# A transformer block on one core: products by half rows, a ninth window slot, a bf16 residual, another start, and an order of issue with tasks that stand back

## The chip, the cores and the metric

The kernel runs on one core of a Trainium2 chip. The core's engines run side by side, each with its own queue of instructions: TensorE (PE, matrix products, with PEld its loading of weights), VectorE (DVE), ScalarE (ACT), GpSimd (POOL) and SyncE (SP, which here issues most of the DMA transfers). The metric is the device time of one execution in microseconds (us). The change is compared with the kernel before by that time.

## The reference, cut to what matters

One block: layer norm, attention over eight earlier positions two apart, output projection and residual, then layer norm, a GELU MLP, bias and residual. The sequence has S = 2048 rows of D = 576 values, 32 heads of 18, and the MLP is F = 4608 wide. All inputs and the output are bf16.

```python
qkv = (ln(x) @ wqkv) -> q, k, v            # (S, 32, 18) each
off = arange(8) * 2                         # this position and 7 earlier ones, 2 apart
logits = einsum("bhsd,bhswd->bhsw", q, k[s - off]) * 18 ** -0.5   # -1e9 where s - off < 0
o = einsum("bhsw,bhswd->bhsd", softmax(logits), v[s - off])
h = x + o @ wo
out = h + gelu(ln(h) @ w1 + b1) @ w2 + b2
```

## The kernel before

**Tiling.** The 2048 rows are cut into 16 tiles of 128: tile j holds the rows p*16 + j, partition p. A step of two positions is therefore a step of two tiles, and a window of eight reaches over all tiles of the same parity, those with a higher j shifted by one partition. The tiles are worked on in the list `ORDER`: the eight even j from 14 down, then the eight odd ones; n is the place in this list.

**Stages of tile n.** `front(n)`: sums for the layer norm (`ln1a`, DVE), the reciprocal root by a power on POOL (`ln1r`), normalisation (`ln1b`, on DVE for n < 8, on ACT after that), transposition (`t1` on PE and `t1e` as copy by ACT for n < 8, `t1e` as DMA transpose on SP's queue after that), then three products with `wqkv` (`c{n}K`, `c{n}V`, `c{n}Q`; line 392), evicted from PSUM by ACT (`e{n}K` ...; line 405) into the windows `kwin[e]`, `vwin[e]` (eight slots for each parity e) or into a `q` buffer. D = 576 is four blocks of 128 rows and a fifth with 64 live rows, the other 64 being zero: a product is 2 halves x 5 blocks = 10 matmuls of 288 columns. K and V of a tile are also written to DRAM (`bw`, lines 425 and 426) and read back one partition lower (`ks`, `vs`, lines 520 and 522) once the tile's own p1a and p2a are done.

`attention(n)` is DVE's: `p1a` (q times the window, line 444), `p1s`, `p1t` and `p1b` (sums over a head, maximum over the slots in three steps, difference), `ex` (ACT's exponential), `p2n` (sum over slots in three steps, reciprocal, weights), `p2a`, `p2s`, `p2b` (weights times values, summed into `o`).

`project(n)`: o is transposed (`t2`: for n < 3 by PE in nine transposes and a copy, otherwise by two DMA transposes on SP's queue), multiplied with `wo` (18 matmuls of 64 rows, two of which run side by side; line 564), evicted as f32 `h`, x is added to it and its sums are taken (`ln2a`), `hb` = h + b2 is put away in bf16, h is normalised on ACT (`ln2b`) and transposed again (`t3`).

`mlp(g)` handles two tiles at once: nine units `u{g}.{u}` on PE (36 matmuls of 64 rows and 256 columns, in pairs; line 630), GELU on ACT (line 641), then four passes of 36 matmuls of 128 rows, `m{g}.{a}.{half}.{u}` in pieces of four (line 667, tile `po`), and `out` on DVE (line 686) with the store `st`. The page names a matmul's shape by its rows: 128*128 or 64*128.

**What sets the order.** Nothing is issued as it is written down. Every step is given to a planner, `Weaver` (line 16), by `add` with its engine, an assumed cost, the steps it comes after, a priority, and buffers that it takes and gives back. `run` (line 35) goes through a simulated time: it always issues next the step that could start earliest, and among equals the one of the lowest priority. So the program is one fixed list for each engine, and an engine does not go past an instruction that waits. PSUM has two buffers for `po` and three (two banks each) for all else.

**The start.** DVE clears the padding of x, of wqkv's last block and of a row of DRAM (lines 274 to 278). Eleven matmuls on idle data (`warm`) come first on PE. The xT tiles lie in parts of the windows that are still free.

Of the kernel before, what the change touches and what calls it, by code (L numbers as in the profile page):

```python
# [15 lines left out]
class Weaver:  # L16
# [4 lines left out]
    def __init__(self, slots):  # L21
        self.tasks = {}
        self.slots = {tag: [0.0] * n for tag, n in slots.items()}
        self.held = {}

    def add(self, name, engine, cost, fn, after=(), prio=0.0, take=None, give=(), lag=0.1, table=None, kb=0.0,
            backlog=2.5, transfers=1):
        assert name not in self.tasks, name
        self.tasks[name] = (engine, cost, fn, tuple(after), prio, take, tuple(give), lag, table,
                            (kb, backlog, transfers))  # L30


    RATE, TABLE, LANES = 240.0, 1.28, 8

    def run(self):
# [8 lines left out]
        table, queue, landed = None, 0.0, [0.0] * self.LANES  # L44
        while left:
            best = None
            for n in ready:
                engine, cost, fn, after, prio, take, give, lag, tab, (kb, backlog, transfers) = left[n]
                start = max([clock.get(engine, 0.0)] + [done[a][2 if done[a][0] == engine else 1] for a in after])
                if take is not None:  # L50
                    tag, key = take
                    if key not in self.held:
                        if not self.slots[tag]:
                            continue
                        start = max(start, min(self.slots[tag]))
                if kb:
                    start = max(start, queue - backlog, landed[transfers - self.LANES - 1])
                rank = (round(start, 3), prio, n)
# [3 lines left out]
            start, _, n = best  # L62
            engine, cost, fn, after, prio, take, give, lag, tab, (kb, backlog, transfers) = left.pop(n)
            ready.discard(n)
            if take is not None and take[1] not in self.held:
                tag, key = take
                free = min(self.slots[tag])
                self.slots[tag].remove(free)
                self.held[key] = tag
            fn()  # L70
            if tab is not None and tab != table:
                cost += self.TABLE
                table = tab
# [8 lines left out]
            for key in give:  # L82
                self.slots[self.held.pop(key)].append(done[n][1])
# [7 lines left out]
def kernel(  # L91
# [37 lines left out]
    dram = ctx.enter_context(tc.tile_pool(name="dram", bufs=1, space=bass.MemoryType.DRAM))  # L129
    ps_po = ctx.enter_context(tc.tile_pool(name="ps_po", bufs=2, space=bass.MemoryType.PSUM))  # L130
    ps_pm = ctx.enter_context(tc.tile_pool(name="ps_pm", bufs=3, space=bass.MemoryType.PSUM))

    kvd = dram.tile([NT, P + 1, 2 * D], BF16, name="kvd")
# [15 lines left out]
    kwin = [wpool.tile([P, W, D], BF16, name=f"kwin{e}") for e in range(2)]  # L149
    vwin = [wpool.tile([P, W, D], BF16, name=f"vwin{e}") for e in range(2)]  # L150
# [10 lines left out]
    def late_pool():  # L161
        if not late:
# [4 lines left out]
    HB, HT, LG, NQ = 4, 9, 4, 13  # L167
# [3 lines left out]
    wv = Weaver({"po": 2, "pm": 3, "oT": 1, "h": 2, "xr": 2, "hb": HB,  # L171
                 "hT": HT, "osb": 2, "hnT": 2, "lg": LG, "prod": 1, "q": NQ})
    add = wv.add
# [3 lines left out]


    TP, TO = 8, 3
    SLACK = 0.6  # L180
    WARM = 11
# [9 lines left out]
    def x_load(n):  # L191
        def fn():
            nc.sync.dma_start(out=T["x", n][:, 0:D], in_=x3[:, ORDER[n], :])
        return fn
# [8 lines left out]
    def wq_rest(eng, t):  # L203
        return lambda: eng.dma_start(out=wqkv_sb[0:64, 4, t * D:(t + 1) * D], in_=A_wqkv[512:576, t * D:(t + 1) * D])
# [30 lines left out]
    Q, K, V = 0, 1, 2  # L235
    for n in range(NT):
        if n < LENT:
            T["x", n] = kwin[1][:].rearrange("p w c -> p (w c)")[:, n * DP:(n + 1) * DP]
        elif n < LENT + XH:
            T["x", n] = hn_bufs[0][:].rearrange("p a b -> p (a b)")[:, (n - LENT) * DP:(n - LENT + 1) * DP]  # L240
        else:
            T["x", n] = early.tile([P, DP], BF16, name=f"x{n}")[:]
        load(f"x{n}", x_load(n), 147, prio=0.1 * n if n else -300)
    for t in (K, V, Q):
        eng, at = (nc.scalar, -200) if t == K else (nc.sync, 0.55 if t == Q else 0.75)
        for r, (part, fn, kb) in enumerate((("a", wq_load(eng, t, 0, 2), 295), ("b", wq_load(eng, t, 2, 4), 295),
                                            ("c", wq_rest(eng, t), 74))):
            add(f"W{t}{part}", "ACT" if t == K else "SP", 0.5, fn, (), at + 0.01 * r, lag=1.8, kb=kb)

    def b2_load():  # L250
        nc.sync.dma_start(out=b2_bc[:], in_=B_b2.partition_broadcast(P))
        nc.sync.dma_start(out=kvd[:, 0, :], in_=w2_sb[0:NT, 0:2, :].rearrange("p a c -> p (a c)"))

    load("b2", b2_load, 150, prio=8.5, issue=0.7, transfers=2)
# [6 lines left out]
    for c in range(W1C):  # L261
        for half in range(2):
            for k in range(0, KC, W1K):
                bulk(f"w1{c}{half}{k}", w1_chunk(c, half, k), 295, prio=20 + c)
    for c in range(W2C):
        bulk(f"w2{c}", w2_chunk(c), 295, prio=30 + c, after=("b2", "b1t", "warm"))
# [5 lines left out]

    for n in range(NT):
        nc.vector.memset(T["x", n][:, D:DP], 0.0)
        if n in (1, 3, 5):
            t = (K, V, Q)[n // 2]
            nc.vector.memset(wqkv_sb[64:128, KT - 1, t * D:(t + 1) * D], 0.0)
    nc.vector.memset(w2_sb[0:NT, 0:2, :], 0.0)


    def warm():
        pw = ps_pm.tile([P, 1024], F32, tag="pm", name="warm")
# [3 lines left out]
    add("warm", "PE", 5.0, warm, (), -400, take=("pm", "warm"), give=("warm",))  # L286

    def b1_turn():
        T["b1T"] = ps_pm.tile([P, 2048], BF16, tag="pm", name="b1T")[:, 0:FT]
# [26 lines left out]
    def transposed(src, shifted=False):  # L316
        starts = [kt * P for kt in range(KT)] + ([64 + kt * P for kt in range(KT - 1)] if shifted else [])
        pt = ps_pm.tile([P, 2048], BF16, tag="pm", name="pt")[:, 0:len(starts) * P]
        pt = pt.rearrange("p (k t) -> p k t", t=P)
        for k, c0 in enumerate(starts):  # L320
            nc.tensor.transpose(pt[:, k, :], src[:, c0:c0 + P], ident[:])
        return pt

    def region(n):
        return n if n < LENT else (0, 1, 2, 3, 0, 1, 0)[n - LENT]


    def front(n):  # L330
# [3 lines left out]
        def ln1a():  # L334
            ln_stats(L1, n, T["x", n][:, 0:D])
            if n >= W:
                ln_var(nc.vector, L1, n, (1.0, EPS))

        def ln1r():
            if n < W:  # L340
# [6 lines left out]
        def ln1b():  # L347
            if n < W:
                nc.vector.tensor_scalar(out=T["x", n][:, 0:D], in0=T["x", n][:, 0:D], scalar1=L1["mv"][:, n, 0:1],
                                        scalar2=L1["rs"][:, n, :], op0=ALU.subtract, op1=ALU.mult)  # L350
            else:
                nc.scalar.activation(out=T["x", n][:, 0:D], in_=T["x", n][:, 0:D], func=ACT.Identity,
                                     scale=L1["rs"][:, n, :], bias=nmr[:, n, :])

        def t1():
            T["pt1", n] = transposed(T["x", n])

        def t1e(by_dma=False):
            if n < 2 * LENT:
                flat = (vwin if n < LENT else kwin)[1][:].rearrange("p w c -> p (w c)")  # L360
                r = region(n)
                T["xnT", n] = flat[:, r * DP:(r + 1) * DP].rearrange("p (k t) -> p k t", k=KT)
            else:
                T["xnT", n] = early.tile([P, KT, P], BF16, name=f"xnT{n}")[:]
            if by_dma:
                nc.sync.dma_start(out=T["xnT", n], in_=T["x", n], transpose=True)
            else:
                nc.scalar.copy(out=T["xnT", n], in_=T["pt1", n])  # L368
# [330 lines left out]
    for g in range(len(GROUPS)):  # L699
        mlp(g)  # L700
# [32 lines left out]
```

## Time and profile before

| | |
|---|---|
| median of 3 runs | 382.62 us (382.17 to 382.9) |
| the profiled execution | 382.82 us, of which its span is 381.0 us |
| PE busy | 373.8 us, 98% of the span |
| DVE busy | 292.5 us, 77% |
| ACT busy | 209.0 us, 55% |
| DMA | 38.48 MB, mean 101 GB/s |
| granted PE clock | 1.00 |

The profile comes from one execution, taken by the hardware. A row gives start, busy time, engine, line of the code, and the tiles written and read; what stands in square brackets is the time that the engine stood idle before it, with what ended it. Matmuls are pipelined and the busy time of a merged row has the drain of its last matmul in it; so the time that a run of matmuls takes on PE is read from its start to the start of the next row. Lines of the chain give start, length and what ran, without brackets. In group rows the numbers after the bar are busy us, mean ns of one, idle us before, and what ended that.

### The profile page before, as it was taken

How to read it: one execution, taken by the hardware profiler on the slowest of the kernel's cores; microseconds unless marked ns; L12 is line 12 of the kernel's file. 1: busy time of each engine (PE TensorE's matmuls, PEld its weight loads, DVE VectorE, ACT ScalarE, POOL GpSimd, SP SyncE). 2: the span in 40 equal slices, each digit the busy share in tenths (PEclk: the TensorE clock that was granted, in tenths of full speed). 3: DMA queues.
4: the chain of work that ended last, by engine and by line, in shares of the span. 5: the costliest groups of instructions: out<-in, count | busy, mean ns of one | idle time of the engine just before them, and what ended most of it. 6: DMA issues, size and time to landing. Idle time of an engine off the chain costs nothing.

```text
span 381.0 us, 10766 instructions
## 1 busy us (share of the span) xinstructions
PE 373.8 (98%) x4618; PEld 304.8 (80%) x4618; DVE 292.5 (77%) x563; ACT 209.0 (55%) x437; POOL 32.4 (9%) x55
## 2 busy tenths in 40 slices
PE   7999999999999999999999999999999999999996
PEld 3777787788788887887788778877887788778874
DVE  7999999899999999999999899998968932010000
ACT  2896665888255762575257526870685088106700
POOL 3670011000110110010001100110011011000000
PEclk9999999999999999999999999999999999999999
DMA  8798999986523212352232333222313331000000
GB/s 254 229 193 273 211 226 236 308 270 199 99 48 101 69 22 64 50 80 62 48 94 64 49 77 82 48 65 61 80 41 56 93 80 25 11 15 19 2 17 15
DMA packets 63967, 38.48 MB, mean 101 GB/s; under 512 B 39520, under 2 KB 63904, under 8 KB 63920
## 3 DMA queue, kind: packets, MB, share of 16 engines
q1 hardware_dynamic: 63296, 37.13, 41.4%
q8 instruction: 36, 0.59, 0.6%
q10 hardware_dynamic: 624, 0.66, 0.5%
q14 instruction: 11, 0.09, 0.1%
HBM read 22.28 MB, written 6.52 MB: 76 GB/s over the span
## 4 chain that ended last, share of the span: by engine, by line
PE 72%; DVE 14%; DMA 2%; issue 1%; POOL 0%; ACT 0%; DVEq 0%; ACTq 0%
PE po L667 35%; PE pm L630 33%; PE pw L564 4%; DVE prod L444 3%; DVE prod L450 2%; DVE prod L485 2%; DMA kwin<-kvd 2%; DVE prod L491 1%; DVE l_st L306 1%; DVE prod L495 1%; DVE h L577 1%; DVE half L437 0%; DVE half L438 0%; DVE hb L590 0%; DVE lg L457 0%
## 5 line engine op out<-in xcount | busy, mean ns | idle before, releaser
L641 ACT ACTIVATE hT<-pm,b_sb 128x256 bf16<-128x256 f32 x288 | 112.5, 477 | 88.6 <-PE pm L630 88.3
L630 PE MATMUL pm<-hnT,w_sb 64*128 64x256 bf16 x2592 | 144.7, 269 | 0.0
L667 PE MATMUL po<-w_sb,hT 128*128 128x288 bf16 x1152 | 142.9, 286 | 0.0
L630 PEld LDWEIGHTS <-w_sb 64*128 64x128 bf16 x2592 | 125.7, 94 | 17.1 <-issue 1.8
L667 PEld LDWEIGHTS <-hT 128*128 128x128 bf16 x1152 | 111.9, 98 | 29.9 <-issue 2.0
L686 DVE TENSOR_TENSOR osb<-po,hb 128x288 bf16<-128x288 f32 x32 | 14.2, 453 | 56.0 <-PE po L667 56.0
L314 POOL TENSOR_TENSOR l_rs<-l_ve,mhalf 128x1 f32<-128x1 f32 x32 | 27.0, 844 | 277.8 <-DVE l_ve L310 277.2
L450 DVE TENSOR_TENSOR prod<-prod 128x2304 bf16<-128x2304 bf16 (+1 forms) x64 | 44.1, 690 | 1.5
L444 DVE TENSOR_TENSOR prod<-kwin,q 128x4608 bf16<-128x4608 bf16 x16 | 40.9, 2555 | 1.3 <-DMA kwin<-kvd 0.9
L485 DVE TENSOR_TENSOR prod<-vwin,at 128x4608 bf16<-128x4608 bf16 x16 | 40.9, 2554 | 0.5 <-ACT vwin L405 0.2
L594 ACT ACTIVATE hn<-h,nmr,l_rs 128x576 bf16<-128x576 f32 (+1 forms) x32 | 19.2, 652 | 23.1 <-issue 13.3
L392 PE MATMUL pq<-wqkv_sb,vwin 128*128 128x288 bf16 x210 | 27.5, 286 | 1.4 <-ACT vwin L368 0.8
L392 PE MATMUL pq<-wqkv_sb,kwin 128*128 128x288 bf16 x210 | 27.1, 286 | 0.0
L392 PEld LDWEIGHTS <-vwin 128*128 128x128 bf16 x210 | 20.1, 98 | 6.9 <-ACT vwin L368 1.2
L392 PEld LDWEIGHTS <-kwin 128*128 128x128 bf16 x210 | 20.2, 98 | 5.4 <-issue 0.5
L491 DVE TENSOR_TENSOR prod<-prod 128x2304 bf16<-128x2304 bf16 x16 | 21.7, 1358 | 0.6
L564 PE MATMUL pw<-wo_sb,oT 64*128 64x288 bf16 x288 | 20.3, 283 | 0.0
L577 DVE TENSOR_TENSOR h<-h,xr 128x576 f32<-128x576 f32 x16 | 12.0, 753 | 10.4 <-ACT h L569 10.4
L569 ACT COPY h<-pw 128x576 f32<-128x576 f32 x16 | 10.5, 654 | 15.4 <-PE pw L564 15.4
L564 PEld LDWEIGHTS <-oT 64*128 64x128 bf16 x288 | 13.6, 94 | 4.3 <-issue 1.2
L405 ACT CAST vwin<-pq 128x576 bf16<-128x576 f32 x16 | 10.2, 641 | 6.9 <-PE pq L392 6.9
L405 ACT CAST kwin<-pq 128x576 bf16<-128x576 f32 x16 | 10.2, 639 | 6.3 <-PE pq L392 6.3
(63 smaller groups left out, 224.8 us busy)
## 6 DMA issues: line engine op xcount, KB each, us to landing
w_sb<-in_B_w_dram SPq DMA_DIRECT2D x36, 288.0 KB, 5.7
xr<-in_A_x_dram SPq DMA_DIRECT2D x16, 144.0 KB, 2.3
out_dram<-osb SPq DMA_DIRECT2D x16, 144.0 KB, 1.9
kvd<-kwin SPq DMA_DIRECT2D x14, 144.0 KB, 4.4
kvd<-vwin SPq DMA_DIRECT2D x14, 144.0 KB, 4.0
kwin<-kvd SPq DMA_DIRECT2D x14, 144.0 KB, 3.0
vwin<-kvd SPq DMA_DIRECT2D x14, 144.0 KB, 2.1
wqkv_sb<-in_A_wqkv_dram SPq DMA_DIRECT2D x4, 288.0 KB, 5.6
```

The source lines that it names most:

```text
L314: nc.gpsimd.tensor_tensor(out=L["rs"][:, n, :], in0=L["ve"][:, n, :], in1=mhalf[:], op=ALU.pow)
L392: nc.tensor.matmul(pq[:, p0:p0 + HALF], lhsT=T["xnT", n][:, kt, :], rhs=wqkv_sb[:, kt, c0:c0 + HALF], start=(kt == 0), stop=(kt == KT - 1))
L405: nc.scalar.copy(out=dst.rearrange("p (d h) -> p d h", h=H), in_=src.rearrange("p h d -> p d h"))
L444: nc.vector.tensor_tensor(out=prod[:], in0=kwin[e][:], in1=T["q", n][:].unsqueeze(1).to_broadcast([P, W, D]), op=ALU.mult)
L450: nc.vector.tensor_tensor(out=pv[:, :, 0:b - a, :], in0=pv[:, :, 0:b - a, :], in1=pv[:, :, a:b, :], op=ALU.add)
L485: nc.vector.tensor_tensor(out=prod[:].rearrange("p w (d h) -> p w d h", d=Dh, h=H), in0=vwin[e][:].rearrange("p w (d h) -> p w d h", d=Dh, ...
L491: nc.vector.tensor_tensor(out=prod[:, 0:4, :], in0=prod[:, 0:4, :], in1=prod[:, 4:8, :], op=ALU.add)
L564: nc.tensor.matmul(pw[:, half, 0:HALF], lhsT=T["oT", n][lo:lo + 64, block(c, half), :], rhs=wo_sb[lo:lo + 64, c, :], start=(c == 0), stop= ...
L594: nc.scalar.activation(out=hn_slots[n % 2][:, c0:c1], in_=src, func=ACT.Identity, scale=L2["rs"][:, n, :], bias=nmr[:, n, :])
L630: nc.tensor.matmul(pm[:, half, q, 0:width], lhsT=w1_sb[lo:lo + 64, c, f0:f0 + P], rhs=T["hnT", g][lo:lo + 64, block(c, half), 0:width], st ...
L641: nc.scalar.activation(out=T["hT", g, u][:, half, q, 0:width], in_=T["pm", g, u][:, half, q, 0:width], func=ACT.Gelu_apprx_tanh, bias=b1_s ...
L667: nc.tensor.matmul(T["po", n, half][:], lhsT=T["hT", g, u][:, r, q, a * P:(a + 1) * P], rhs=w2_sb[:, ft, half * HALF:(half + 1) * HALF], s ...
```

## The change

*Rows in halves.* The fifth block of x transposed is filled twice, rows 512 to 575 in both halves of the partitions, and so is wqkv's. A product is eight matmuls of 128 rows and two of 64, which run side by side. A product begins with whichever shape PE used last (`flip`). For n >= 8 the duplicate columns are fetched by two DMAs (`dup`). A transposition by PE writes its last block in two column halves of 64.

*Ninth slot.* One tensor of 17 slots holds both parities; the slot in the middle is common. K and V of a tile are copied within SBUF into the neighbouring slot, one partition on; the bounce through DRAM goes, p1a and p2a are split in two where the slot left out lies between the others. The maximum and the sum over the slots are one reduction each.

*bf16 residual.* `h` is bf16, b2 is added to it in place, after `ln2b`, and seven buffers of it replace two and four.

*First two tiles.* x1 is loaded by ACT's queue; x0's variance is on DVE, its normalisation and its copies are in two parts, its products go block by block. x1's sums come before x0's normalisation on DVE.

*PSUM and places.* `px`, a fourth double buffer, serves t1 and products until all products are done, and then becomes the two `po` buffers. The units wait for all products. The xT tiles lie in the end of `w2_sb`, so loads of w2 wait for products. A DMA transposition waits for the Q product five tiles back (`AHEAD`).

*Table.* `HOLD` names 59 steps and a time for each, by which `run` regards them as later when it compares, without delaying their simulated start. The planner also charges 0.055 for a change of shape on PE.

```diff
-    RATE, TABLE, LANES = 240.0, 1.28, 8
+    RATE, SWITCH, LANES = 240.0, {"ACT": 1.28, "PE": 0.055}, 8
...
-                rank = (round(start, 3), prio, n)
+                rank = (round(start + self.hold.get(n, 0.0), 3), prio, n, start)
...
+            tab = tab or {"PE": "128"}.get(engine)
+            if tab == "flip":
+                tab = "128" if table["PE"] == "64" else "64"
+            if tab is not None and tab != table.get(engine):
+                cost += self.SWITCH[engine]
...
+    kwin = wpool.tile([P, 2 * W + 1, D], BF16, name="kwin")
+    vwin = wpool.tile([P, 2 * W + 1, D], BF16, name="vwin")
+
+    def slot(e, s):
+        return 2 * W - s if e else s
+
+    def ranges(e, s):
+        if e:
+            return [(2 * W - s, 2 * W + 1), (W, 2 * W - s - 1)]
+        return [(0, s + 1), (s + 2, W + 1)]
...
+    HOLD = {
+        "x14": 0.8, "x15": 0.8, "W2a": 0.8, "b2": 0.8, "b1": 2.5, "w1116": 2.5, "w1200": 2.5, "w1203": 0.4,
+        "w1213": 0.4, "b1t": 0.4, "t3p1": 4, "vs2": 4, "ln2m2": 0.8, "ln2b2": 2.5, "t3p2": 7, "ln1b3": 0.4, "e3Q": 0.8,
+        "p1b3": 12, "ks3": 4, "hb3": 12, "ln2m3": 0.4, "ln2b3": 2.5, "p2n4": 1.5, "wo4": 2.5, "ln2r4": 2.5,
+        "p1b5": 0.4, "ex5": 4, "ln2b5": 12, "e6K": 0.4, "p1a6": 1.5, "ex6": 12, "p2b6": 12, "ex7": 7, "ln2a7": 2.5,
+        "e8K": 0.4, "e8Q": 0.4, "p1s8": 12, "ln1r9": 4, "ln1r10": 1.5, "t1e10": 0.8, "p1s10": 4, "p1t10": 7,
+        "ln1b12": 0.8, "t1e13": 1.5, "c2Q": 0.4, "c10K": 4, "c14V": 2.5, "c14Q": 2.5, "c15Q": 12, "out0.1": 0.8,
+        "m0.1.0.7": 12, "u1.4": 4, "out2.1": 12, "m1.1.0.8": 12, "u2.7": 4, "u2.8": 4, "m2.0.1.7": 4, "m2.1.0.7": 7,
+        "m2.1.1.5": 7,
+    }
+    wv = Weaver({"po": 2, "pm": 3, "px": 1, "oT": 1, "h": HB, "xr": 2,
...
-    WARM = 11
+    WARM, AHEAD = 10, 5
...
+            (nc.scalar if n == 1 else nc.sync).dma_start(out=T["x", n][:, 0:D], in_=x3[:, ORDER[n], :])
...
-    for n in range(NT):
-        nc.vector.memset(T["x", n][:, D:DP], 0.0)
-        if n in (1, 3, 5):
-            t = (K, V, Q)[n // 2]
-            nc.vector.memset(wqkv_sb[64:128, KT - 1, t * D:(t + 1) * D], 0.0)
-    nc.vector.memset(w2_sb[0:NT, 0:2, :], 0.0)
+    for win in (kwin, vwin):
+        nc.vector.memset(win[0:1, W, :], 0.0)
...
+        for k in range(KT - 1):
+            nc.tensor.transpose(pt[:, k, :], src[:, k * P:(k + 1) * P], ident[:])
+        for lo, c0 in ((0, D - 64), (64, tail)):
+            nc.tensor.transpose(pt[lo:lo + 64, KT - 1, :], src[:, c0:c0 + 64], ident[:])
...
+                for c0, c1 in ((0, D),) if n else ((0, 2 * P), (2 * P, D)):
+                    x = T["x", n][:, c0:c1]
+                    nc.vector.tensor_scalar(out=x, in0=x, scalar1=L1["mv"][:, n, 0:1], scalar2=L1["rs"][:, n, :],
+                                            op0=ALU.subtract, op1=ALU.mult)
...
+        add(f"ln1b{n}", "DVE" if n < W else "ACT", 0.38 if n < W else 0.8, ln1b,
+            [f"ln1r{n}"] + ([dups[n]] if n in dups else []) + (["ln1a1"] if n == 0 else []), prio=-20 + n)
...
+            load(f"t1e{n}", lambda: t1e(True), 164, [f"ln1b{n}", f"c{n - AHEAD}Q"], prio=-20 + n, issue=1.2, lag=3.0)
...
+    def project_in(n, t):
+        def fn():
+            pq = banks(f"pq{label(n, t)}", [1024], F32)
+            T["pq", n, t] = pq
+            blocks = [(half, kt, 0, P) for half in range(2) for kt in range(KT - 1)]
+            if n == 0:
+                blocks.sort(key=lambda b: b[1])
+            rest = [(half, KT - 1, 64 * half, 64 * half + 64) for half in range(2)]
+            todo = rest + blocks if wv.table["PE"] == "64" else blocks + rest
+            seen = {0: 0, 1: 0}
+            for half, kt, lo, hi in todo:
+                c0, p0 = t * D + half * HALF, 512 - HALF + half * HALF
+                nc.tensor.matmul(pq[:, p0:p0 + HALF], lhsT=T["xnT", n][lo:hi, kt, :],
+                                 rhs=wqkv_sb[lo:hi, kt, c0:c0 + HALF], start=(seen[half] == 0),
+                                 stop=(seen[half] == KT - 1))
+                seen[half] += 1
...
+        add(f"c{label(n, t)}", "PE", 1.115, fn, [f"t1e{n}"] + [f"W{t}{part}" for part in "abc"], prio=prio,
+            take=(("pm", "px"), f"pq{label(n, t)}"), lag=0.3, table="flip")
...
+        def over_slots(dst, src, op):
+            nc.vector.tensor_reduce(out=dst[:], in_=src[:].rearrange("p w h -> p h w"), axis=AX.X, op=op)
...
+            for lo, hi in ranges(e, s):
+                if hi > lo:
+                    nc.vector.tensor_tensor(out=prod[:, at:at + hi - lo, :], in0=kwin[:, lo:hi, :],
+                                            in1=T["q", n][:].unsqueeze(1).to_broadcast([P, hi - lo, D]), op=ALU.mult)
+                at += hi - lo
...
+        if s:
+            def shift(win):
+                a, b = slot(e, s), slot(e, s + 1) if s + 1 < W else W
+                return lambda: nc.sync.dma_start(out=win[1:P, b, :], in_=win[0:P - 1, a, :])
+
+            for c, win, last in (("K", kwin, "p1a"), ("V", vwin, "p2a")):
+                load(f"{c.lower()}s{n}", shift(win), 146, prio=-5,
+                     after=[f"e{n}{c}"] + ([f"{last}{n - 1}"] if n else []) + ([f"{c.lower()}s{n - 1}"] if s + 1 < W else []))
...
-            T["h", n] = sb.tile([P, D], F32, tag="h", name="h")
+            T["h", n] = sb.tile([P, D], BF16, tag="h", name="h", bufs=HB)
...
-            T["hb", n] = sb.tile([P, D], BF16, tag="hb", name="hb", bufs=HB)
-            nc.vector.tensor_tensor(out=T["hb", n][:], in0=T["h", n][:], in1=b2_bc[:], op=ALU.add)
+            nc.vector.tensor_tensor(out=T["h", n][:], in0=T["h", n][:], in1=b2_bc[:], op=ALU.add)
...
+            deps = [f"t3{n}" for n in ns] + ["b1e"] + w1s[2 * u * P // CW] + w1s[(2 * u + 1) * P // CW] + (last or products)
...
+    add("pos", "-", 0.0, pos, qkv_done, take=("px", "pos"), lag=0.0)
```

## The prediction

> **What bounds the kernel now.** First the page's busy shares, the span in slices, and the chain.
>
> ```profile
> PE 373.8 (98%) x4618; PEld 304.8 (80%) x4618; DVE 292.5 (77%) x563; ACT 209.0 (55%) x437; POOL 32.4 (9%) x55
> ...
> PE   7999999999999999999999999999999999999996
> ...
> PE 72%; DVE 14%; DMA 2%; issue 1%; POOL 0%; ACT 0%; DVEq 0%; ACTq 0%
> ```
>
> TensorE (PE) is full from the second slice to the last. The chain has VectorE (DVE) links only before 104 us, and in that stretch PE found other work, so the time is PE's queue: when its stream starts, what it holds, its holes, and 3.4 us behind the last matmul (377.6 to 381.0). Hence PE in order of time, row start to row start, since busy time includes the drain of the last matmul.
>
> ```profile
> 32.42 7.51 PE L392 MATMUL pq<-wqkv_sb,vwin 128*128 128x288 bf16 x60
> 39.77 0.67 PE L321 MATMUL pt<-ident,o 128*128 128x128 bf16 x9
> 40.28 2.61 PE L392 MATMUL pq<-wqkv_sb,kwin 128*128 128x288 bf16 x20
> 42.82 1.27 PE L564 MATMUL pw<-wo_sb,oT 64*128 64x288 bf16 x18
> 44.03 8.75 PE L392 MATMUL pq<-wqkv_sb,kwin 128*128 128x288 bf16 x70
> ```
>
> Sixty product matmuls take 7.35 us: 122.5 ns each, 1.225 us for a product of ten. The twenty from 40.28 should end at 42.73; the output projection, in 64-row tiles, starts at 42.82: 0.09 us lost on entering. Its eighteen matmuls run in nine pairs, and the next 128-row matmul follows after 1.21 us. The chain shows what they cost between tasks of their own shape:
>
> ```profile
> 135.39 17.75 PE po L667 x144
> 153.14 11.89 PE pm L630 x216
> 165.03 1.10 PE pw L564 x18
> ...
> 172.03 1.09 PE po L667 x8
> 173.12 1.21 PE pw L564 x18
> 174.33 16.77 PE po L667 x136
> ```
>
> 1.10 us among 64-row tasks, 1.21 next to 128-row ones; eight po matmuls take 1.09 where 0.98 was due, 136 take 16.77 where 16.66 was due. So a change of tile shape costs 0.09 to 0.11 us, either way. This row decides the case.
>
> Then the holes, and the start:
>
> ```profile
> 5.71 0.43 DVE L349 TENSOR_SCALAR kwin<-kwin,l_mv,l_rs 128x576 bf16<-128x576 bf16 x1 [0.95 <-POOL l_rs L314]
> ...
> 7.60 1.40 PE L392 MATMUL pq<-wqkv_sb,vwin 128*128 128x288 bf16 x10 [0.78 <-ACT vwin L368]
> ...
> 9.82 0.45 PE L321 MATMUL pt<-ident,kwin 128*128 128x128 bf16 x5 [0.55 <-DVE kwin L349]
> ...
> 28.75 2.61 PE L392 MATMUL pq<-wqkv_sb,vwin 128*128 128x288 bf16 x20 [0.55 <-ACT vwin L405]
> ...
> 103.67 0.79 PE L321 MATMUL pt<-ident,hn 128*128 128x128 bf16 x9 [0.59 <-ACT hn L594]
> ```
>
> The first product starts at 7.60. Its stream to 377.64 holds 48 products (58.8 us), 72 MLP units of 1.965 (141.5), 1152 second-layer matmuls (141.1), 16 projections (17.6), and transposes (5): 364 of 370 us. The holes shown are about 2, the rest is changes of shape.
>
> **The change, part by part, in PE time.** The sum is made against the profiled execution's 382.82 us (span 381.0, 1.8 around it), which is 0.2 above the median of 382.62.
>
> *Rows in halves.* Each product's last block, 64 live rows of 128, becomes two half-row matmuls side by side: 9 slots for 10, 48 x 0.1225 = 5.9 saved. Against that each product now has one change of shape inside it, since a product starts in the shape in which the last task ended: 48 x 0.10 = 4.8. Among the first eight tiles a transpose in 128 rows comes between products, so the return is paid too: 8 x 0.10 = 0.8. The projections at 42.8 and 59.8 can now stand beside a half-row end, and the last product can end in the units' shape: -0.5. The changes can't cost less than nothing, which would leave -5.9; the highest row, 0.11, gives 0.6 more. I take 0.10, since three kinds of neighbours agree on it.
>
> [...]
>
> *Transposes* of a tile get one slot more, at 0.28/5 = 0.056 us: 14 x 0.056 = 0.8. That their last block goes out in two 64-column halves has no row of its own: between nothing and two changes of shape each, 0.2. I take nothing, since the rows show only changes of the row count; the other end is a rival. Sum so far -5.9 + 4.8 + 0.8 - 0.5 + 0.8 = 0.0: **PE's work stays as it is**.
>
> *First two tiles.* x0's sums cannot start earlier: x tiles land 3.2 us or more after issue, and DVE began at 3.77 as its memsets (gone now) ended, so those hid nothing. The variance moves from POOL (0.19 and two hand-overs) to DVE (0.15); the power (0.55) would end at about 5.5 for 5.67. But x1's sums (1.05 us) now stand ahead of x0's normalisation on DVE, which starts at about 6.05 for 5.71. With it in two halves, transposes and copies in two, the first product starts at about 7.15, ends at 8.35 for 8.83, and tile 1's follows at about 9.6 for 10.32. I take -0.7. If x1, now on ACT's queue, lands late, DVE waits with x0 behind it, and the gain is 0; without that wait it is 1.1. One warm-up matmul less changes nothing while x0 isn't ready (they end 0.4 earlier).
>
> *Fourth PSUM buffer* while the products run: the hole before 28.75 waits for an eviction. ACT has about 0.07 us more work on each of the eight tiles that it normalises (640 columns for 576), so I take -0.4, between -0.87 (50 matmuls from 21.76 end at 27.88) and 0.5 longer. *u0* and *po* now wait for all products; they did so before (u0 at 75.23, behind the last one), so 0.
>
> *Ninth slot, bf16 residual, one reduction for three operations.* All DVE and DMA:
>
> ```profile
> L577 DVE TENSOR_TENSOR h<-h,xr 128x576 f32<-128x576 f32 x16 | 12.0, 753 | 10.4 <-ACT h L569 10.4
> ...
> L590 DVE TENSOR_TENSOR hb<-h,b_bc 128x576 bf16<-128x576 f32 x16 | 12.0, 749 | 0.0
> ...
> L496 DVE TENSOR_TENSOR o<-prod 128x576 bf16<-128x576 bf16 x16 | 7.3, 459 | 1.1 <-DVE prod L495 0.5
> ```
>
> The two adds go to the bf16 add's 0.46 (-0.6 a tile); each maximum and sum over slots was 0.29 + 0.23 + 0.19 plus gaps, 0.80, and becomes one reduction over 256 f32 values, nearest row the difference lg<-lg,mx of that size, 0.43 (-0.7 a tile, for the two); the split p1a and p2a add 0.06 to 0.16 each. About -1.1 us a tile, 17 in all. DVE ends at 316 and PE at 377, so nothing of it counts directly. It counts where PE waited for this chain: the hole before 103.67 goes (-0.6). The next wait behind it is group 1's first unit at 115.16, for which tile 3's DMA transposes were issued until 113.9: some 0.7 spare, and four tiles' 1.1 move it ahead by more than PE moves. The bounce through DRAM (28 writes, 28 reads) becomes 28 copies within SBUF, a shift that no longer waits for its own tile's p1a: DVE's 0.94 wait for kwin goes, off the path.
>
> *Table of tasks that stand back.* It changes order, not work. Projections inside a 128-row pass (101.8, 173.1) cost two changes each; if they are moved to a border, -0.4, else 0; I take -0.4. What is late next is tile 8's transpose on SP's queue, which now waits for tile 3's Q product; four Q products, 4 x 1.2 = 4.8, lie between it and tile 8's K.
>
> ```profile
> DMA to landing us min/median/max: 3.2/4.8/6.5
> ```
>
> With the median it is just in time, with the longest 1.7 late; behind it on SP stand only loads due later. I take +0.2.
>
> Sum: 0.0 - 0.7 - 0.4 - 0.6 - 0.4 + 0.2 = -1.9, so 380.9 against 382.82; less the 0.2 to the median, **380.7 us** (-0.5%), own range 379.2 to 382.2 by the bounds above.
>
> **Rivals.**
> *The changes inside products are half hidden.* The planner charges 0.055. For it: the half-row weights use one half of the array, and might be loaded early. Against: the projection's do too, and it pays 0.09. 56 changes x 0.045 = 2.5 less: 378.2.
> *Halved transposes change shape as well* (slower). Eight of x: into the column halves and out again; six of o and hn the same: 28 changes at the upper row's 0.11 = 3.1, and 0.6 for the others at 0.11: 384.3. It decides from about 2.7 us of it on. Against: PE has holes near x's transposes that may take some. For: the array is cut anew, by columns.
> [...]
> *Nothing that counts:* tile 8's transpose lands 1.5 late, and the early gain is given back as one wait of PE before K8: 382.2.
> *Starvation at a group's border:* tasks stood back (p1b3 and hb3 by 12) bring tile 3 to group 1 late; 385 or more if it is 4 us. Against: DVE's shorter tiles.
>
> **How the numbers follow.** Forecast 0.45, half hidden 0.25, halved transposes 0.15, nothing 0.10, starvation 0.05. 0.2% (0.76 us) is about what a measurement tells from no change: faster is below 381.85, slower above 383.4. Faster: 0.40 of the forecast's, 0.25, 0.02 = 0.67. Slower: 0.13 + 0.05 + 0.01 of the third = 0.19. The rest, 0.14, is the same. The range is 377.0 to 384.3: it leaves out the lower end of the half-hidden case and what lies above the second rival, under 0.2. The likeliest sign's own range is 377.0 to 381.8.
>
> **What would show it.** Two products in a row on PE: start to start 2.4 us for a pair (forecast), 2.3 (half hidden), 2.45 before. A transpose of x to the next product: 0.34 or 0.54. First product at about 7.15, tile 1's at 9.6. No hole before a transpose of hn near 100. A wait of PE on the DMA for tile 8 near 39 us would show the third. The prediction is wrong if the MLP part (units, 37.7 us per group) changes, if a first product runs at the slow clock (PE's first transposes took 0.31 us, later ones 0.22; a product would cost 1.1 more), or if u1 waits.

## The result and the profile after

The changed kernel takes 451.38 us in the median (450.87 to 451.94), beside 382.76 us for the kernel before: a ratio of 1.1796, 95% interval 1.1776 to 1.1817. That is 18% slower where 0.5% faster was forecast. The profiled execution takes 451.53 us, span 449.7. Further down, one execution of the kernel with whole transposes and one of the kernel with two more warm-up matmuls, the profiled ones, took 991.2 and 780.6 us, with the MLP's matmuls 2.7 and 2.1 times as long at a recorded granted clock of 1.00; no row below is from them, the ranges leave them out, and the medians move by about 0.1 us with them.

The page of the changed kernel: busy shares, PE and the granted clock in 40 slices, and the chain.

```profile
PE 395.3 (88%) x4631; PEld 302.4 (67%) x4631; DVE 280.2 (62%) x500; ACT 208.7 (46%) x435; POOL 32.8 (7%) x62
...
PE   6988495999945999999596999999999999989996
...
PEclk9898887799976999999988899999999999999999
...
PE 67%; DMA 19%; DVE 6%; SPq 6%; issue 1%; ACT 1%; ACTq 0%
```

PE is no longer full: it has holes in the first 24 slices, the clock is lower around long ones (0.76 between 40 and 60 us), and a fifth of the chain is DMA, where it was 2% before. Of the 68.7 us by which the span grew, 47.2 are idle time of PE (54.4 us for 7.2) and 21.5 are busy time (395.3 for 373.8), which goes with the lower granted clock: 0.72 between 120 and 140 us, where it was 1.00 before. DVE's busy time fell by 12.3 us, as foreseen in kind. PE in order of time shows where the holes are (start, busy time, what ran, and in brackets the idle time before it):

```profile
8.08 1.15 PE L489 MATMUL pm<-wqkv_sb,w_sb 128*128 128x288 bf16 x8
11.73 0.30 PE L489 MATMUL pm<-wqkv_sb,w_sb 64*128 64x288 bf16 x2 [2.50 <-DMA wqkv_sb<-in_A_wqkv_dram]
...
56.59 2.46 PE L489 MATMUL pm<-wqkv_sb,w_sb 128*128 128x288 bf16 x10 [6.57 <-DMA w_sb<-hnT]
...
77.20 2.46 PE L489 MATMUL pm<-wqkv_sb,w_sb 128*128 128x288 bf16 x10 [4.97 <-DMA w_sb<-xs]
...
102.30 13.93 PE L707 MATMUL pm<-hnT,w_sb 64*128 64x256 bf16 x252
...
129.84 4.00 PE L744 MATMUL pm<-w_sb,hT 128*128 128x288 bf16 x16 [5.46 <-DMA w_sb<-in_B_w_dram]
```

The first product stops before its last two matmuls for 2.5 us, because wqkv's last block isn't there. The MLP's first unit starts at 102.30. In the kernel before it was:

```profile
75.23 13.93 PE L630 MATMUL pm<-hnT,w_sb 64*128 64x256 bf16 x252
```

Group 0 then takes until 158.08 (55.8 us for 40.0); 11.0 of it is waiting for w2. So 27.1 of the 68.7 us come up to the first unit, 15.8 in group 0, and the rest behind. The chain names what was slow (start, length):

```profile
1.66 10.03 DMA wqkv_sb<-in_A_wqkv_dram
...
45.19 11.35 DMA w_sb<-hnT
...
115.97 12.80 DMA vwin<-vwin
```

The second is a DMA transpose of an x tile, issued behind such copies. The transfers in the last of these windows, the changed kernel between 118.6 and 125 us in 40 slices, with what they moved (a DMA digit of 0 is less than a tenth of the 16 engines):

```profile
DMA  0000000000000000000000000000068799789999
GB/s 22 22 29 22 29 22 22 29 22 29 22 22 29 22 29 22 22 29 22 22 29 22 22 22 29 22 29 22 29 130 130 245 324 303 173 238 434 338 338 353
```

While a copy of 127 rows is under way, about 24 GB/s flow and the 16 engines are busy for 0.07 of the time (118.6 to 122.5 us), which is about one of them; as soon as others get through, 130 to 434. Where all 16 engines are busy (a digit of 9), 303 to 434 flow; a sixteenth of that is 19 to 27, so 24 GB/s is about what one engine moves. Such a copy is 127 x 1152 B = 146 KB, so 6.1 us at that rate. The one issued at 115.97 took 12.8; another had been issued at 110.25, and two take 12.2 (that the second waited for the first is argued from this sum). Between 10 and 12 us, while loads of wqkv's last block are under way, the same view mostly stands at 46 GB/s, twice as much, with 0.14 of the engines' time (10.5 to 11.5 us), about two of them: there the outermost dimension of the load is two copies.

SP's own issue stops too. From the changed kernel's order of time on SP:

```profile
115.97 0.69 SPq L598 DMA_DIRECT2D vwin<-vwin  x1
116.70 5.89 SPq L652 DMA_DIRECT2D xr<-in_A_x_dram  x1
122.65 3.20 SPq L278 DMA_DIRECT2D w_sb<-in_B_w_dram  x4
```

Issuing the load of x takes 5.89 us. Before, it took (shortest, median, longest in ns):

```profile
L573 SPq DMA_DIRECT2D xr<-in_A_x_dram x16: 337/430/1352, 37.9 to 300.5; - x16
```

The four loads of w2 that PE waits for at 124.4 are issued behind it.

A last loss is in the MLP alone, in every group, here the last one:

```profile
426.48 5.08 PE L744 MATMUL pm<-w_sb,hT 128*128 128x288 bf16 x40
432.11 4.57 PE L744 MATMUL pm<-w_sb,hT 128*128 128x288 bf16 x36 [0.55 <-DVE osb L763]
437.22 4.57 PE L744 MATMUL pm<-w_sb,hT 128*128 128x288 bf16 x36 [0.55 <-DVE osb L763]
442.35 4.08 PE L744 MATMUL pm<-w_sb,hT 128*128 128x288 bf16 x32 [0.55 <-DVE osb L763]
```

A pass has 36 matmuls. The stop comes after 40: the next pass does its first piece of four and then waits until DVE has read the pass before, although that lies in the other half of the tile. This takes 14.5 us in 20 places: 19 stops of about 0.55 and one of 4.1, at which DVE was late with other work as well.

### The profile page after: what moved, and what is told of

Read it like the earlier page. It is cut to its first block, busy times and chain, and to the rows that moved or that the text cites. A ratio compares the mean times of both kernels' runs of the same rounds, so it can differ in the third digit from the quotient of the medians.

```text
span 449.7 us, 10666 instructions
## 1 busy us (share of the span) xinstructions
PE 395.3 (88%) x4631; PEld 302.4 (67%) x4631; DVE 280.2 (62%) x500; ACT 208.7 (46%) x435; POOL 32.8 (7%) x62
## 4 chain that ended last, share of the span: by engine, by line
PE 67%; DMA 19%; DVE 6%; SPq 6%; issue 1%; ACT 1%; ACTq 0%
PE pm L744 30%; PE pm L707 26%; PE pm L489 6%; PE pm L643 4%; DMA oT<-o 4%; DMA w_sb<-in_B_w_dram 3%; DMA vwin<-vwin 3%; DMA w_sb<-hnT 3%; SPq L269 3%; DMA wqkv_sb<-in_A_wqkv_dram 2%; DVE osb L763 2%; DMA hnT<-in_A_x_dram 2%; DMA w_sb<-xs 2%; SPq L278 2%; DVE l_st L368 1%
## 5 line engine op out<-in xcount | busy, mean ns | idle before, releaser
L744 PE MATMUL pm<-w_sb,hT 128*128 128x288 bf16 x1152 | 152.2, 293 | 25.5 <-DVE osb L763 14.5
L489 PE MATMUL pm<-wqkv_sb,w_sb 128*128 128x288 bf16 (+1 forms) x480 | 68.2, 309 | 18.3 <-DMA w_sb<-hnT 6.6
L489 PEld LDWEIGHTS <-w_sb 128*128 128x128 bf16 (+1 forms) x480 | 41.0, 103 | 43.5 <-issue 17.0
L763 DVE TENSOR_TENSOR osb<-pm,h 128x288 bf16<-128x288 f32 x32 | 14.2, 455 | 85.6 <-PE pm L744 85.6
L559 DVE TENSOR_TENSOR prod<-vwin,at 128x4032 bf16<-128x4032 bf16 (+7 forms) x30 | 41.8, 1433 | 0.4
L515 DVE TENSOR_TENSOR prod<-kwin,q 128x4032 bf16<-128x4032 bf16 (+7 forms) x30 | 41.7, 1429 | 0.1
L648 ACT CAST h<-pm 128x576 bf16<-128x576 f32 x16 | 10.5, 657 | 43.5 <-PE pm L643 43.5
L643 PE MATMUL pm<-wo_sb,oT 64*128 64x288 bf16 x288 | 21.7, 293 | 5.0 <-DMA oT<-o 5.0
L672 ACT ACTIVATE hn<-h,nmr,l_rs 128x576 bf16<-128x576 bf16 (+1 forms) x29 | 18.2, 674 | 12.2 <-DVE nmr L664 6.4
L368 DVE BATCH_NORM_STATS2 l_st<-h 128x6 f32<-128x288 bf16 x32 | 13.1, 452 | 0.6
```

Source lines behind the costliest of these rows:

```text
L489: nc.tensor.matmul(pq[:, p0:p0 + HALF], lhsT=T["xnT", n][lo:hi, kt, :], rhs=wqkv_sb[lo:hi, kt, c0:c0 + HALF], start=(seen[half] == 0), sto ...
L515: nc.vector.tensor_tensor(out=prod[:, at:at + hi - lo, :], in0=kwin[:, lo:hi, :], in1=T["q", n][:].unsqueeze(1).to_broadcast([P, hi - lo, ...
L559: nc.vector.tensor_tensor(out=prod[:, w0:w1, :].rearrange("p w (d h) -> p w d h", d=Dh, h=H), in0=vwin[:, lo:hi, :].rearrange("p w (d h) - ...
L643: nc.tensor.matmul(pw[:, half, 0:HALF], lhsT=T["oT", n][lo:lo + 64, block(c, half), :], rhs=wo_sb[lo:lo + 64, c, :], start=(c == 0), stop= ...
L744: nc.tensor.matmul(T["po", n, half], lhsT=T["hT", g, u][:, r, q, a * P:(a + 1) * P], rhs=w2_sb[:, ft, half * HALF:(half + 1) * HALF], star ...
L763: nc.vector.tensor_tensor(out=T["osb", n][:, c0:c0 + HALF], in0=T["po", n, half], in1=T["h", n][:, c0:c0 + HALF], op=ALU.add)
```

## The experiments

The theory had three causes: copies over 127 rows that go through one DMA engine (24 GB/s), the load of wqkv's last block that goes through two (46 GB/s), and two accumulators that are kept in one PSUM tile. The rivals were the gating of the DMA transposes and of the w2 loads, and the table.

**Shift copies in two.** Planner and order of issue unchanged.

```diff
-                return lambda: nc.sync.dma_start(out=win[1:P, b, :], in_=win[0:P - 1, a, :])
+                def fn():
+                    for lo, hi in ((0, 112), (112, P - 1)):
+                        nc.sync.dma_start(out=win[lo + 1:hi + 1, b, :], in_=win[lo:hi, a, :])
+                return fn
```

> The changed kernel with one edit: each shift copy within SBUF (rows 0 to 126 to rows 1 to 127) is issued as two, 112 rows and 15 rows. Order of issue and all else as it was. Theory A (a copy whose row count of 127 has no common divisor with the 16 DMA engines goes through one engine at about 23 GB/s, lands 6 to 13 us late, and holds up what stands behind it): the copies land in 2 to 5 us, the products end at about 80 to 85 us instead of 102, the waits of PE for loads of w2 (11 us) and for oT in group 2 (some 14 us) go, and the execution takes 395 to 410 us. Theory B (the waits come from where the steps were put: transposes that wait for the Q product five tiles back, loads of w2 that wait for products, tasks that stand back): it stays at 430 us or more.

405.34 us, 46 us less, in one execution. The products end at 77.98, the waits for w2 and oT are gone. The copies of kwin land in 2.0 to 6.5 us, 4.5 in the median. The gating is the same in this run, so it wasn't the cause of these 46 us. Nor is it that the copies begin at partition 1: the ones of 112 rows begin there too.

**The last block of wqkv as two loads.** In the line taken out, `src` is two copies of 64 rows, the copies outermost.

```diff
...
-            eng.dma_start(out=wqkv_sb[:, KT - 1, t * D:(t + 1) * D], in_=src)
+            for lo in (0, 64):
+                eng.dma_start(out=wqkv_sb[lo:lo + 64, KT - 1, t * D:(t + 1) * D], in_=A_wqkv[D - 64:D, t * D:(t + 1) * D])
```

> The changed kernel with one edit: the load of wqkv's last block into both halves of the partitions, one DMA with a leading dimension of two copies, is issued as two DMAs of 64 rows. Theory A (two copies outermost means two of the 16 engines, at 46 GB/s, 10 us to land): K's block lands by about 6 us, the first product is not cut in two by a wait of 2.5 us, x7 to x9 load earlier; but the shift copies are still the later limit, so the whole takes 443 to 448 us instead of 451. Theory B (the load is late because it shares the engines with x and the other blocks of wqkv): no change, 450 to 452 us.

447.2 us, 4.2 less, in one execution: by theory A. The first product isn't cut in two any more.

**Two PSUM tiles for po.** A tile each from the start, without px.

```diff
-                        T["po", n, half] = T["pos"][:, wv.spot[f"po{n}.{half}"][1], 0:HALF]
+                        T["po", n, half] = ps.tile([P, HALF], F32, tag=f"po{...}", name="po")[:]
```

> The changed kernel with the two accumulators of the second MLP layer as two PSUM tiles of one bank each from the start, instead of two halves of one tile in the px buffer; products then have three PSUM buffers. Theory A (the halves of one tile are kept apart in space but not by the waits: the next pass waits, after its first four matmuls, for DVE to have read the other half): the stops of 0.5 us before po matmuls, 14.5 us in 20 places, go, and the time falls by 13 to 15 us, to 436 to 439 us. Theory B (PE waits for the eviction because DVE is late): the stops stay, 450 us or so.

436.27 us, 15.1 less, in one execution, as theory A had it, and PE waits for `osb` nowhere any more. But the size is not clean. Without px the order moved too: PE does all nine units of group 0 in a row, then waits 5.5 us for GELU and, further on, 7.1 for oT, while the 11.0 for w2 are gone. That the wait was for the tile, not for DVE's speed, is shown by the run below that keeps the order.

**The three together.**

> The three edits together (shift copies in two, last block of wqkv in two loads, two PSUM tiles for po). If the three causes are all of it, PE is the limit again and its queue decides: products that cost as much as before (one slot less, one change of tile shape more), transposes that cost 0.2 us more each, a start as early as before: 379 to 386 us. If something else in the change is slow as well (the gating of the DMA transposes, the table), it stays above 390 us.

403.23 us, ratio 1.0542 (1.0523 to 1.0561): not the 379 to 386 expected. PE's order of time in this run shows new holes:

```profile
100.66 9.93 PE L747 MATMUL po<-w_sb,hT 128*128 128x288 bf16 x56 [5.49 <-ACT hT L721]
...
127.12 0.61 PE L382 MATMUL pm<-ident,hn 128*128 128x128 bf16 x4 [6.51 <-ACT hn L675]
```

Taking px away had changed what the planner sees, and so the order. PE does all nine units in a row (324 matmuls from 77.32) and then waits for GELU, as in the run before. The edit had moved two things. So the next run kept px and its order.

**The three together, order kept.** px lies in a pool of its own, which is closed after the last product; po gets two tiles in its place.

```diff
+    px_cm = tc.tile_pool(name="px", bufs=1, space=bass.MemoryType.PSUM)
+    px = px_cm.__enter__()
...
-        T["pos"] = banks("pos", [2, 512], F32)
+        px_cm.__exit__(None, None, None)
+        T["pos"] = ctx.enter_context(tc.tile_pool(name="po", bufs=1, space=bass.MemoryType.PSUM))
```

> The changed kernel with the three causes taken away and its order of issue kept as it is: shift copies as 112 and 15 rows, the last block of wqkv as two loads of 64 rows, and px given back after the products so that po gets two tiles of a bank each in its place. In the run before, px was taken away altogether, which changed the planner's order, and new waits of 5.5 and 6.5 us appeared at 95 and 120 us. Theory A (three causes, and the order is good): e1_shift's 405 less 14.6 us of stops at po, less 2 to 4 us at the start: 385 to 389 us, with no wait over 2 us on PE behind 30 us. Theory B (the order of issue is bad in itself): 395 us or more, with waits of 5 us at the borders of groups.

384.06 us, ratio 1.0028 (1.0009 to 1.0046), a little below the range. The three causes together make 67 of the 69 us. PE waits nowhere for DMA or for `osb`, and behind 8 us for nothing (all of PE's list of waits: us in total, times, longest):

```profile
PE pm L349 <- DVE w_sb L339: 1.2, 1, 1.2
PE pm L386 <- DVE kwin L421: 0.6, 1, 0.6
PE pm L434 <- DVE kwin L421: 0.5, 1, 0.5
```

**Without the table**, on top of that (`wv.hold = HOLD` left out).

> The run with the three causes taken away, without the table of tasks that stand back (the planner then takes the earliest start alone). If the table repairs an order that makes PE wait, it is slower than with the table by 2 us or more, with waits of PE near the borders of groups. If the table moves nothing that PE waits for, it is within 1 us. If the table itself brings steps late, it is faster by 2 us or more.

387.48 us, ratio 1.0123 (1.0095 to 1.0152): 3.4 us slower by the medians, about 4 at equal granted clock (as in the next experiment). PE waits 1.25 us for tile 8's transpose at 42.7 (`w_sb<-hnT`, the wait that the prediction had named), 0.5 for hn at 54, 0.8 for evictions of po, 0.7 for GELU. In this kernel the table repairs the order.

**Products always in one order.**

```diff
-            todo = rest + blocks if wv.table["PE"] == "64" else blocks + rest
+            todo = blocks + rest
```

> The run with the three causes taken away, with each product always in the order 128-row blocks, then the half rows, whatever shape came before: two changes of tile shape a product for one, up to 48 more. Theory A (a change of shape costs 0.10 to 0.12 us of PE and nothing hides it): 4 to 6 us slower than the run with flips. Theory B (half hidden, 0.055): 2 to 3 us slower. If the products' part is not limited by PE: no difference.

387.47 us, ratio 1.0131 (1.0102 to 1.0161): 3.4 us slower, between the two theories. Compared at equal mean granted clock, the difference is 4.0, the lower edge of theory A: 386.7 against 382.7 at 1.00, and 388.2 against 384.2 at about 0.996 (the profiled execution with flips, 385.52, stands apart). The profile settles it. Six products in a row, with flips (first fence) and without (second):

```profile
37.14 7.41 PE L492 MATMUL pm<-wqkv_sb,w_sb 64*128 64x288 bf16 x60
44.48 0.40 PE L386 MATMUL pm<-ident,o 128*128 128x128 bf16 x4
```

```profile
36.03 7.96 PE L492 MATMUL pm<-wqkv_sb,w_sb 128*128 128x288 bf16 x60
43.92 0.40 PE L386 MATMUL pm<-ident,o 128*128 128x128 bf16 x4
```

7.34 and 7.89 us; the four products from 26.26 to 31.09 with flips give 1.21 each, those without 1.315. One change of shape costs 0.105 us of PE, and nothing hides it.

**Whole transposes.** The last block in one transposition of 128 columns; DVE and ACT write the 64 duplicate columns, in lines that are left out here.

```diff
-        for k in range(KT - 1):
+        for k in range(KT):
             nc.tensor.transpose(pt[:, k, :], src[:, k * P:(k + 1) * P], ident[:])
-        for lo, c0 in ((0, D - 64), (64, tail)):
-            nc.tensor.transpose(pt[lo:lo + 64, KT - 1, :], src[:, c0:c0 + 64], ident[:])
...
```

> The run with the three causes taken away, with the last block of each transposition on PE as one of 128 columns instead of two of 64; the 64 duplicate columns are written by DVE and ACT as a short instruction more. Theory A (the column halves are changes of tile shape, 0.11 us each, two a transposition, beside one slot more): 14 transpositions take 0.2 us less each, 2 to 3 us faster. Theory B (they cost a slot alone, 0.056 us): 0.8 us faster or less.

382.43 us, ratio 1.0001 (0.9986 to 1.0015): 1.6 us less, the whole of what had remained, though the intervals of the two runs just overlap. That lies between the theories; the rows speak for column halves that change the shape. With halves, t2's ten took from 44.48 to 45.22 in the run with the three causes taken away, 0.74 us; whole, in the last run of this section, its nine take 0.51, as in the kernel before (39.77 to 40.28):

```profile
42.43 0.45 PE L386 MATMUL pm<-ident,o 128*128 128x128 bf16 x5
42.72 0.39 PE L389 MATMUL pm<-ident,o 128*128 128x128 bf16 x4
42.94 1.37 PE L489 MATMUL pm<-wqkv_sb,w_sb 128*128 128x288 bf16 x10
```

**127 rows in the kernel before.** Nothing else of the change.

```diff
-            load(f"ks{n}", lambda: nc.sync.dma_start(out=kwin[e][:, s, :], in_=kvd[n, 0:P, 0:D]),
+            load(f"ks{n}", lambda: nc.sync.dma_start(out=kwin[e][1:P, s, :], in_=kvd[n, 1:P, 0:D]),
```

(and the same for V)

> The kernel before with one edit: the reads that bring K and V back from DRAM one partition lower take rows 1 to 127 instead of all 128 (row 0 holds positions that are masked). Nothing else of the change is in it. Theory A (127 rows go through one DMA engine): the 28 reads land in 6 to 13 us instead of 2 to 3, hold up the queue behind them, and DVE and PE wait for windows: 10 to 60 us slower. Theory B (what was slow in the changed kernel was copying within SBUF, from a partition to its neighbour): no change, within 1 us of 382.4.

444.17 us in one execution, 61.6 more than the kernel before beside it. One row less in 28 reads makes the kernel 16% slower, and these reads come from DRAM: it doesn't take copying within SBUF. DVE's two large products now wait for their windows (groups by line):

```profile
L444 DVE TENSOR_TENSOR prod<-kwin,q 128x4608 bf16<-128x4608 bf16 x16 | 40.9, 2558 | 24.3 <-DMA kwin<-kvd 24.0
L485 DVE TENSOR_TENSOR prod<-vwin,at 128x4608 bf16<-128x4608 bf16 x16 | 40.9, 2555 | 26.0 <-DMA vwin<-kvd 25.7 <-ACT vwin L405 0.2
```

In the kernel before they had waited 1.3 and 0.5 us:

```profile
L444 DVE TENSOR_TENSOR prod<-kwin,q 128x4608 bf16<-128x4608 bf16 x16 | 40.9, 2555 | 1.3 <-DMA kwin<-kvd 0.9
L485 DVE TENSOR_TENSOR prod<-vwin,at 128x4608 bf16<-128x4608 bf16 x16 | 40.9, 2554 | 0.5 <-ACT vwin L405 0.2
```

**119 rows**, the same reads: 9 to 127, so rows 1 to 8 of each shifted tile are left out and the output is not the block's.

> The kernel before with its 28 reads from DRAM one partition lower cut to 119 rows, 9 to 127; rows 1 to 8 of each shifted tile are not brought, so the output there is not the reference's. 119 is 7 x 17. Theory A (the number of engines is the largest divisor of the row count up to 16): seven engines, the reads land in 3 to 5 us, and the time is 382 to 386 us. Theory B (every row count that is not a multiple of 16 goes through one engine): as with 127 rows, 435 to 450 us.

384.02 us beside 381.9, one execution each: by theory A, and far from the 444 of 127 rows. From 123.9 to 124.4 us, where by its bytes the read of vwin issued at 122.27 is under way, 158 to 173 GB/s flow at 4 to 5 tenths of the 16 engines; seven times 24 is 168. The same read of 128 rows, in the kernel before, reaches 302 at 9 tenths. The 2 us can't be put down to the 119 rows: executions of the kernel before alone spread over 1.8 us, this one's first product ran at a granted clock of 0.50 (8 to 10 us, 1.00 before), and PE's waits for DMA come to 0.5 us.

**Two more warm-up matmuls**, on the run with whole transposes (`WARM` 12 for 10).

> The run with the three causes taken away and whole transposes, with 12 warm-up matmuls on idle data instead of 10. In the profile of the run with the three causes taken away PE idles from 5.6 to 6.1 and 7.0 to 7.7 us, its first product takes 2.4 us instead of 1.2, and full speed comes at about 14 us. Theory A (the warm-up is one matmul too short, and the slow clock at the start costs 1.5 to 2.5 us in some executions): times lie closer together, about 381.6 us, 0.2% faster than before. Theory B (the slow start has to do with when the execution began): no change, 382.4 us.

381.85 us, ratio 0.9983 (0.9974 to 0.9992): the fastest kernel of the study, 0.17% below the kernel before. Its times lie between 381.58 and 382.46, where those of the run with whole transposes reached 383.4. That fits theory A; no row of this run shows its start.

**Tile 1's transposes behind tile 0's K product**, on top of that.

```diff
-            add(f"t1{n}", "PE", 0.34, t1, [f"ln1b{n}"], prio=-60, ...
+            add(f"t1{n}", "PE", 0.34, t1, [f"ln1b{n}"] + (["c0K"] if n == 1 else []), prio=-60, ...
```

> The same with tile 1's transposes issued behind tile 0's K product instead of ahead of it. Theory A (the first product waits for nothing but tile 1's turn on PE): it starts at about 7.4 us instead of 8.4, and the whole takes 0.5 to 1 us less than the run with 12 warm-up matmuls: 380.7 to 381.2 us. Theory B (the order behind it, which the table was made for, falls out of step): 383 us or more, with a wait of PE near the borders of groups.

382.33 us, ratio 0.9997 (0.9988 to 1.0005): between the two theories. The first product does start early, and the gain is given back twice:

```profile
7.33 1.38 PE L489 MATMUL pm<-wqkv_sb,w_sb 128*128 128x288 bf16 x10 [0.46 <-ACT w_sb L444]
...
13.63 0.45 PE L386 MATMUL px<-ident,kwin 128*128 128x128 bf16 x5 [0.97 <-DVE kwin L419]
...
51.61 3.80 PE L489 MATMUL pm<-wqkv_sb,w_sb 128*128 128x288 bf16 x30 [1.25 <-DMA w_sb<-xs]
```

PE is ahead of DVE's normalisation at 13.6 and of a DMA transpose at 51.6. The second wait is the kind that the prediction feared for tile 8.

## Why the prediction was wrong

**The step that failed** is the one on the ninth slot: "The bounce through DRAM (28 writes, 28 reads) becomes 28 copies within SBUF", put down as DVE and DMA only, "off the path". It counted the transfers and not their shape. The copies before took 128 rows, these take 127. They were priced by nothing, their landing by no row, and no rival dealt with them. Undone alone it gives 46 us; done alone in the kernel before it costs 62. The hint was in the diff: `win[1:P]`, and no transfer before had a row count other than 128, 64, 36, 32 or 16; those that the profile times landed in 2 to 8 us.

What the views show of the row count: 127 rows go at 24 GB/s with about one of the 16 engines busy, a load with two copies outermost at 46 with about two, and 119 = 7 x 17 rows at 158 to 173, harmless as far as one execution can tell. What sets the number of engines is not shown beyond these counts.

**Not in the sum at all** was the load of wqkv's last block: 4.2 us. The prediction's start of the first product takes wqkv for landed and gives no reason.

**"*u0* and *po* now wait for all products; they did so before ... so 0"** looked at when po may start and not at how its two halves are kept apart. One tile with two readers in turn gave a stop of 0.55 us at the border of most passes, 14.5 us in all with the one of 4.1. That the wait goes with the tile is shown by the run with two tiles and the order kept; that it is put there when the program is built, as `out` is issued behind the next pass's first piece, is argued from the 40 matmuls.

**Rows in halves: right.** 1.1025 + 0.10 was forecast for a product, 1.21 measured, and the half-hidden rival is refuted by 0.105 us for each further change. The two holes that were to go, before 28.75 and before 103.67, are right too: with the three causes taken away PE's list has no such wait.

**Transposes: mis-sized, by the second rival's mechanism.** 0.34 us and 0.56 were taken for t1 and t2, at a slot more each; t1 takes 0.51 (17.48 to 17.99 in the run with the three causes taken away), t2 0.74. The term of 0.8 was 14 x 0.23 = 3.2; the time gives 1.6 of it back when they are whole.

**The start: the order was missed.** DVE was even earlier than worked out (x0's normalisation at 5.68, not 6.05), but PE's order has tile 1's transposes ahead of the first product. It starts at 8.0 to 8.5, not 7.15. With the order exchanged it starts at 7.33, and waits later take that back.

**The table** was taken at -0.4, for projections moved to a border. They are not moved: with the three causes taken away they still stand inside passes (104.86 and 177.37). What the table is worth there, 3.4 us by the medians, are waits that PE has without it. Whether it does harm in the order without px (403 us) is not shown, since no run has that order without the table.

**DVE's work** fell by 12.3 us for the 17 forecast: a reduction over slots takes 0.59 us where 0.43 was taken. As said, none of it counted.

With the three causes taken away and whole transposes, the kernel takes what it took before, 382.4, and not 380.7. That it comes out even bears "PE's work stays as it is" out only in part: the extra cost of the transposes was taken out by a further edit, the holes are gone, and the start came no earlier. It is a balance of several terms.

## What to carry to other kernels

Before costing a moved or reshaped transfer by its bytes, read the row count of its outermost dimension: here 112 + 15 rows cost next to nothing, while 127 rows took 6 us at 24 GB/s and held up what was issued behind. An accumulator that one engine fills while another reads its neighbour wants a tile of its own, not half of one, which cost 14.5 us here. An edit that takes a buffer away can move the whole order of issue, as taking px away did, so an experiment on such a kernel has to keep the order or say that it moved.

## What the runs showed that was not expected

*A slow copy stops the issuer.* SP spent 5.89 us on issuing one load of x, and 10.3 us on six loads of w1 from 34.85, while copies of 127 rows were under way. With the copies in two, each load of xr up to 123 us is issued in 0.54 to 0.60 us, and the six loads of w1 in 4.28. Why the issue itself is held up is not shown.

*The clock at the start.* In the run with the three causes taken away the warm-up ends at 5.6 us, PE idles twice for half a microsecond, and the first product goes at little more than half speed:

```profile
8.45 2.46 PE L492 MATMUL px<-wqkv_sb,w_sb 128*128 128x288 bf16 x10
10.84 0.61 PE L386 MATMUL pm<-ident,kwin 128*128 128x128 bf16 x4
```

2.39 us for ten matmuls, 1.32 in the run without flips, whose order is the same up to there; the prediction had named this sign, at 1.1 us more. The record of the granted clock stands at 1.00 there, so the slow clock is argued from the matmuls alone; in the run with wqkv's block in two loads the same product takes 2.39 us too, and the record shows 0.50 (8 to 10 us). Only some executions seem to have it: without any change this kernel took 382.64 to 385.52 us. With two more matmuls on idle data the times lie closer together (381.58 to 382.46 us, up to 383.4 without them); that this comes from the clock is the author's estimate, as no trace of that run shows the start.
